# Attention and two feed-forward layers on one Trainium2 core: which PSUM banks the later pairs' flips, spreads and weighted sums use, and which engine subtracts the reloaded inputs' low parts

## The chip, the cores and the metric

One core of a Trainium2 chip runs the whole program. The metric is device time in microseconds (us); of the kernel before, three runs took 1277.73, 1278.05 and 1278.85 us, median 1278.05.

## What is computed

For 4 batches of 12 heads, 448 positions and 64 channels: q and k are normalised (RMS norm with gains), scores = q k^T / 8, softmax over the keys, times v. The result, 1792 tokens of 768 channels, goes through two layers. The first is x @ w_in (to 2048), relu, g = s * r * r + b, g @ w_out (back to 768). The second is h = x @ w_in, g = h * cos(h), g @ w_out.

```
attn = softmax(scale * rmsnorm(q) @ rmsnorm(k).T); x = attn @ v
x = (s * relu(x @ w1_in)**2 + b) @ w1_out
h = x @ w2_in; out = (h * cos(h)) @ w2_out
```

All inputs and outputs are float32; the layers' weights are stored as 64-bit floats and turned into 32-bit floats by bit operations in the kernel. Each operand of the layers' products is split in a high and a low part, and three matmuls (high by high, high by low, low by high) give one product.

## The kernel before, in words

Attention goes by pairs of heads: 24 pairs, six to a batch. A pair has four steps, one for each quarter of the queries (112 of 448). A step makes two score tiles, one per head (`scores`, L223): VectorE takes the negative maximum of each (L246), ScalarE the exponential (L254). Two steps later `turn` (L264) transposes the weights into two tiles that ScalarE (first head, L278) and VectorE (second head, L276) copy out. Once in a pair, `flip` (L190) transposes the next pair's normalised q (in the pair's second step) and k (third step), copied out in `unflip` by ScalarE (L211) and VectorE (L213); and for the pair before, in the third step, `spread` (L280) transposes the reciprocal sums into a tile that ScalarE copies (L286), and `mix` (L288) makes the weighted sum of v in 16 matmuls, which VectorE multiplies by the spread in `finish` (L303) a step later.

PSUM has eight banks, and each of these tiles takes one: two under the tag "mo", which the layers' matmuls use too (hidden tiles ph, output tiles po), two under "tp" and four under "sc". A tile waits till the tile that had its bank has been read. For the first nine pairs (`ALONE` = 9) attention runs alone, and flip, spread and sum take "mo"; from the tenth on the first layer's matmuls run between the steps and take "mo" for themselves, and `bank` (L185) sends flip, spread and sum to "tp", beside the turned weights. (A flip made for pair i asks `bank` with i - 2.) A score tile of step s also waits for the exponentials of step s - 2 by a dependency of its own (`follow`). TensorE's attention work is kept in the order in which it is written (`line`); all else is ordered by the compiler's list of priorities and its own estimate of times, so an order of instructions on an engine is fixed when the kernel is built.

The first layer is done in two passes: batches 0 and 1 while attention for the rest goes on, then batches 2 and 3. The attention output of batches 2 and 3 is written to DRAM and loaded again by `reload` (L576) when the weights come round: six column blocks of 128 x 448 for each batch. One block is a DMA into a tile xr of tag "t0" (two slots, shared with the hidden tiles' relu results), a cast on ScalarE to the high part xh (L98), and a subtraction that gives the low part xl (L99), both in `split` (L95). The subtraction is on VectorE for blocks 0, 1, 4 and 5 and on GpSimd for 2 and 3. The first layer's result for batches 0 and 1 is reloaded for the second layer in the same way. VectorE also converts the weights (L439 to L441), scales the squares (L479) and adds the output tiles into their accumulators (L525); GpSimd squares (L477) and makes most of the other low parts (L494, L401, L220).

Of the kernel before, what the change touches and what calls it, by code (L numbers as in the profile page):

```python
# [10 lines left out]
F32 = mybir.dt.float32  # L11
# [22 lines left out]
def body(ctx, tc, q, k, v, g_q, g_k, w1_in, w1_out, s_in, b_in, w2_in, w2_out, out):  # L34
    nc = tc.nc
# [3 lines left out]
    P = 128  # L39
# [53 lines left out]
    xs = {}  # L93

    def split(src, pool, key, eng=nc.gpsimd):  # L95
        hi = pool.tile([P, S], F32R, tag="xh", name=f"xh_{key}", bufs=2 * NE)
        lo = pool.tile([P, S], F32R, tag="xl", name=f"xl_{key}", bufs=2 * NE)
        nc.scalar.copy(hi, src)  # L98
        eng.tensor_tensor(lo, src, hi.bitcast(F32), ALU.subtract)  # L99
        return hi, lo  # L100
# [12 lines left out]
    def attention(keep):  # L113
        att, ps = pools["att"], pools["ps"]
# [70 lines left out]
        def bank(i, name):  # L185
            if i < ALONE:
                return psm.tile([P, 512], F32, tag="mo", name=name, bufs=2)
            return ps.tile([P, 512], F32, tag="tp", name=name)

        def flip(i, nm):  # L190
            b, hp = pairs[i]
            pt = bank(i - 2, f"pt_{nm}_{b}_{hp}")[:, :S]
            src = st[i]["q by chunk"] if i == 0 and nm == "q" else st[i]["n" + nm]
            mm = [nc.tensor.transpose(pt[:, c * CP:(c + 1) * CP], src[:, c, :, :].rearrange("p h d -> p (h d)"), ident[:CP, :CP]) for c in range(NCH)]
            line("PE", mm[0], mm[-1])
            st[i]["p" + nm] = pt
# [83 lines left out]
        def spread(i):  # L280
            b, hp = pairs[i]
            rt = bank(i, f"rt_{b}_{hp}")[:, :S]
            mm = [nc.tensor.transpose(rt[:, c * CP:(c + 1) * CP], st[i]["rb"][:, c, :, :].rearrange("p h d -> p (h d)"), ident[:CP, :CP]) for c in range(NCH)]
            line("PE", mm[0], mm[-1])
            x = st[i]["x"] = att.tile([P, S], F32, tag="xf", name=f"xf_{b}_{hp}")
            line("ACT", nc.scalar.copy(x, rt))  # L286

        def mix(i, part):  # L288
            b, hp = pairs[i]
            if part[0] == 0:  # L290
                st[i]["pa"] = bank(i, f"av_{b}_{hp}")[:, :S]
            mm = []
            for kc in part:
                for j in range(2):
                    mm.append(nc.tensor.matmul(st[i]["pa"][j * D:(j + 1) * D, :], st[i]["v"][:, j, kc, :], st[i]["pT", j][:, kc, :], start=(kc == 0), stop=(kc == NCH - 1)))  # L295
            line("PE", mm[0], mm[-1])
            for z in mm[1:]:
                issue_after(z, mm[0])
# [277 lines left out]
    def reload(layer, b, c, pool):  # L576
        t = ma.tile([P, S], F32, tag="t0", name=f"xr_{layer}_{b}_{c}")
        nc.sync.dma_start(t, stash[layer, b, c])
        xs.setdefault((layer, b), []).append(split(t, pool, f"{layer + 1}_{b}_{c}", nc.vector if c % 4 < 2 else nc.gpsimd))

    segs = [(0, (0,), [0]), (0, (0, 1), range(1, NCK)), (0, (1,), [0]), (0, (2, 3), range(NCK)), (1, (0, 1, 2, 3), range(NCK))]
    L2 = 4
# [69 lines left out]
    for n, u in enumerate(units):  # L652
# [14 lines left out]
        if soon:  # L667
            reload(*soon.pop(0))
        elif again and n % 4 == 0:
            reload(*again.pop(0))  # L670
        if u[0] == "in":
            while soon and len(xs.get((u[1], u[5]), [])) < NE:
                reload(*soon.pop(0))
            while again and u[1] == 1:
                reload(*again.pop(0))
        for cost in (unit_in if u[0] == "in" else unit_out)(*u[1:]):
            debt += cost * rates[min(seg, 1)]
            while debt > 0:
                c = next(steps, None)
# [34 lines left out]
```

## Time and profile before

| | |
|---|---|
| median of three runs | 1278.05 us |
| the profiled execution's own time | 1284.1 us |
| its span | 1282.3 us |
| TensorE busy | 1245.4 us (97%) |
| VectorE busy | 861.2 us (67%) |
| ScalarE busy | 757.0 us (59%) |
| GpSimd busy | 619.8 us (48%) |
| mean granted TensorE clock | 0.995 |

The profile is of one execution. Its times count from the first instruction. "PE" is TensorE, "PEld" its weight loads, "DVE" VectorE, "ACT" ScalarE, "POOL" GpSimd, "SP" the engine whose queue issues the DMAs. In a timeline a row is one or several like instructions: start, time taken, engine, line, operation, out<-in, and in square brackets how long the engine had stood and what ended that. Matmuls overlap, so their times add up to more than the time that passes; the distance of their starts is the better measure. A granted clock of 1.00 is 2.4 GHz, one of 0.50 is 1.2 GHz.

### The profile page before, as it was taken

The numbers are of one execution on the slowest core, as the hardware profiler recorded it, in microseconds if no ns is written. First come the engines' busy times: TensorE is split into PE (matmuls) and PEld (weight loads), VectorE is DVE, ScalarE is ACT, GpSimd is POOL, SyncE is SP. The second block draws the span as 40 slices with busy tenths as digits, with TensorE's granted clock in tenths as the row PEclk, the third lists the DMA queues.
The fourth block names the chain that finished last, engine by engine and source line by source line (L and its number), as shares of the span: only waits on it lengthen the run. The fifth ranks groups of instructions, "written<-read, shape, count | busy, mean of one in ns | idle before, by whom it ended". The sixth has DMA issues, their size and how long they took to land.

```text
span 1282.3 us, 19021 instructions
## 1 busy us (share of the span) xinstructions
PE 1245.4 (97%) x6788; PEld 1051.2 (82%) x6788; DVE 861.2 (67%) x1456; ACT 757.0 (59%) x1704; POOL 619.8 (48%) x673
## 2 busy tenths in 40 slices
PE   7999998999999999999999999999999999999998
PEld 5544676678777776789999999998999999999998
DVE  6888768876877866743444447854767766676755
ACT  5778878766666655525332226787656657565640
POOL 5566857565474642424332223665443535354531
PEclk9999999999999999999999999999999999999999
DMA  4333324533443322542221212211212111111205
GB/s 128 97 97 105 113 79 127 167 122 117 151 119 112 120 89 71 158 145 86 92 64 50 62 45 74 74 39 59 61 41 74 50 50 50 50 50 50 62 1 173
DMA packets 82223, 111.34 MB, mean 87 GB/s; under 512 B 8112, under 2 KB 72144, under 8 KB 82128
## 3 DMA queue, kind: packets, MB, share of 16 engines
q1 hardware_dynamic: 82128, 110.13, 28.3%
q8 instruction: 53, 0.87, 0.3%
q14 instruction: 42, 0.34, 0.1%
HBM read 86.51 MB, written 23.59 MB: 86 GB/s over the span
## 4 chain that ended last, share of the span: by engine, by line
PE 58%; DVE 10%; ACT 7%; DMA 2%; POOL 2%; issue 2%; DVEq 0%; ACTq 0%; POOLq 0%
PE ph L464 24%; PE po L543 14%; PE po L516 14%; PE av L295 2%; DVE t L440 2%; PE tp L272 2%; DVE gt L488 2%; DVE gt L489 2%; PE sc L233 2%; DVE t L441 1%; DMA xr<-xd 1%; ACT gh L493 1%; ACT gt L490 1%; DVE c L439 1%; DVE gt L479 1%
## 5 line engine op out<-in xcount | busy, mean ns | idle before, releaser
L464 PE MATMUL ph<-xl,wh 128*128 128x448 f32 x768 | 283.0, 369 | 0.0
L464 PE MATMUL ph<-xh,wl 128*128 128x448 f32 x768 | 283.0, 368 | 0.0
L464 PE MATMUL ph<-xh,wh 128*128 128x448 f32 x768 | 280.4, 370 | 0.5 <-ACT r L475 0.5
L494 POOL TENSOR_TENSOR gl<-gt,gh 128x448 fp32r<-128x448 f32 x128 | 152.7, 1197 | 177.4 <-ACT gh L493 177.3
L516 PE MATMUL po<-gh,wh 128*128 128x448 f32 x384 | 146.8, 384 | 9.8 <-DVE acc L525 8.4
L401 POOL TENSOR_TENSOR wl<-t,wh 128x384 fp32r<-128x384 f32 x128 | 140.4, 1111 | 32.5 <-ACT wh L398 31.3
L464 PEld LDWEIGHTS ph<-xl,wh 128*128 128x128 f32 x768 | 144.2, 188 | 14.0 <-issue 2.0
L464 PEld LDWEIGHTS ph<-xh,wh 128*128 128x128 f32 x768 | 144.1, 188 | 13.8 <-issue 1.3
L543 PE MATMUL po<-wh,gh 128*128 128x384 f32 x448 | 152.0, 340 | 2.4 <-ACT acc L549 1.2
L464 PEld LDWEIGHTS ph<-xh,wl 128*128 128x128 f32 x768 | 144.3, 188 | 12.2 <-issue 1.0
L398 ACT CAST wh<-t 128x384 fp32r<-128x384 f32 x200 | 95.2, 512 | 97.5 <-PE po L516 48.7
L525 DVE TENSOR_TENSOR acc<-po,acc 128x448 f32<-128x448 f32 x168 | 102.8, 618 | 74.2 <-PE po L516 73.7
L543 PE MATMUL po<-wl,gh 128*128 128x384 f32 x448 | 149.8, 335 | 0.4 <-POOL wl L401 0.4
L543 PE MATMUL po<-wh,gl 128*128 128x384 f32 x448 | 149.8, 334 | 0.0
L551 DVE TENSOR_TENSOR acc<-po,acc 128x384 f32<-128x384 f32 x196 | 105.3, 550 | 61.0 <-PE po L543 61.0
L254 ACT ACTIVATE pr<-sc,top 112x448 f32<-112x448 f32 x184 | 116.2, 637 | 49.1 <-DVE top L246 48.6
L516 PE MATMUL po<-gl,wh 128*128 128x448 f32 x384 | 142.8, 372 | 0.0
L516 PE MATMUL po<-gh,wl 128*128 128x448 f32 x384 | 142.7, 372 | 0.0
L492 POOL TENSOR_TENSOR gt<-hs,gt 128x448 f32<-128x448 f32 x64 | 78.5, 1227 | 128.7 <-ACT gt L491 113.6
L493 ACT CAST gh<-gt 128x448 fp32r<-128x448 f32 x128 | 71.2, 564 | 96.0 <-DVE gt L479 57.0
L477 POOL TENSOR_TENSOR r<-r 128x448 f32<-128x448 f32 x64 | 65.7, 1027 | 125.5 <-ACT r L475 118.6
L440 DVE SCALAR_TENSOR_TENSOR t<-c,t 128x384 uint32<-128x384 uint32 x128 | 96.2, 755 | 38.7 <-ACT t L436 35.8
(101 smaller groups left out, 2386.2 us busy)
## 6 DMA issues: line engine op xcount, KB each, us to landing
raw<-in_moe_w_in_dram SPq DMA_DIRECT2D x64, 384.0 KB, 3.5
raw<-in_moe_w_out_dram SPq DMA_DIRECT2D x64, 384.0 KB, 3.2
t<-wd SPq DMA_DIRECT2D x72, 192.0 KB, 2.4
wd<-t SPq DMA_DIRECT2D x64, 192.0 KB, 2.7
rawk<-in_k_dram SPq DMA_DIRECT2D x24, 224.0 KB, 3.5
rawv<-in_v_dram SPq DMA_DIRECT2D x24, 224.0 KB, 2.9
rawq<-in_q_dram SPq DMA_DIRECT2D x23, 224.0 KB, 3.0
xd<-xf SPq DMA_DIRECT2D x12, 224.0 KB, 2.6
```

The lines of the kernel that those rows point to most:

```text
L254: e = line("ACT", nc.scalar.activation(pr, sc[j], AF.Exp, bias=tops[j], scale=scale[j], accum_out=st[i]["sums"][:, c, j:j + 1]))
L398: z = nc.scalar.copy(wh, w)
L401: eng.tensor_tensor(wl, w, wh.bitcast(F32), ALU.subtract)
L440: nc.vector.scalar_tensor_tensor(t, c, 0x80000000, t, ALU.bitwise_and, ALU.bitwise_or)
L464: nc.tensor.matmul(h, a, m, start=(c == 0 and n == 0), stop=(c == NE - 1 and n == 2))
L492: nc.gpsimd.tensor_tensor(gt, h, gt, ALU.mult)
L493: nc.scalar.copy(gh, gt)
L494: nc.gpsimd.tensor_tensor(gl, gt, gh.bitcast(F32), ALU.subtract)
L516: marks["out"] = nc.tensor.matmul(po, a, m, start=(f == 0 and n == 0), stop=(f == CF - 1 and n == 2))
L525: nc.vector.tensor_tensor(at, po, at, ALU.add)
L543: nc.tensor.matmul(po, a, m, start=(f == 0 and n == 0), stop=(f == CF - 1 and n == 2))
L551: nc.vector.tensor_tensor(at, po, at, ALU.add)
```

## The change

`bank` gives flips, spreads and weighted sums from the tenth pair on a tile of the tag "sc", in the same ring of four as the scores, instead of one of the tag "tp"; the "tp" ring keeps the turned weights alone. `reload` gives the low parts to VectorE only for the second layer; for the first layer's second pass (batches 2 and 3) all six blocks go to GpSimd.

```
         def bank(i, name):
             if i < ALONE:
                 return psm.tile([P, 512], F32, tag="mo", name=name, bufs=2)
-            return ps.tile([P, 512], F32, tag="tp", name=name)
+            return ps.tile([P, 512], F32, tag="sc", name=name, bufs=4)
...
     def reload(layer, b, c, pool):
         t = ma.tile([P, S], F32, tag="t0", name=f"xr_{layer}_{b}_{c}")
         nc.sync.dma_start(t, stash[layer, b, c])
-        xs.setdefault((layer, b), []).append(split(t, pool, f"{layer + 1}_{b}_{c}", nc.vector if c % 4 < 2 else nc.gpsimd))
+        xs.setdefault((layer, b), []).append(split(t, pool, f"{layer + 1}_{b}_{c}", nc.vector if layer and c % 4 < 2 else nc.gpsimd))
```

## Rows read from the trace of the kernel before

**Rows 1.** The page: busy time by engine, and the exponentials' group.
```profile
PE 1245.4 (97%) x6788; PEld 1051.2 (82%) x6788; DVE 861.2 (67%) x1456; ACT 757.0 (59%) x1704; POOL 619.8 (48%) x673
...
L254 ACT ACTIVATE pr<-sc,top 112x448 f32<-112x448 f32 x184 | 116.2, 637 | 49.1 <-DVE top L246 48.6
```

**Rows 2.** Windows: stretch, length, busy time (instructions) by engine, clock, DMA share, GB/s.
```profile
160.00:200.00 40.00, 39.01 (x242) 28.88 (x240) 26.19 (x46) 29.23 (x73) 20.55 (x29) 1.00 0.27 82
200.00:240.00 40.00, 34.12 (x179) 25.39 (x179) 36.42 (x58) 30.08 (x76) 29.91 (x30) 0.91 0.55 172
...
520.00:560.00 40.00, 36.03 (x169) 29.75 (x169) 24.83 (x38) 14.10 (x29) 14.89 (x14) 0.96 0.54 170
```

**Rows 3.** Waits of TensorE, whole span: us in total, times, longest.
```profile
PE po L516 <- DVE acc L525: 8.4, 9, 2.2
...
PE sc L233 <- ACT pr L254: 3.0, 2, 2.3
```

**Rows 4.** Timeline of TensorE: four stalls of spread, sum and turned weights.
```profile
150.96 0.60 PE L283 MATMUL rt<-ident,rb 112*128 112x112 f32 x4 [1.03 <-DVE pT L276]
...
195.16 3.23 PE L295 MATMUL av<-pT,rawv 112*64 112x448 f32 x16 [0.42 <-DVE pT L276]
...
220.66 0.60 PE L283 MATMUL rt<-ident,rb 112*128 112x112 f32 x4 [3.14 <-DVE pT L276]
...
233.00 0.60 PE L272 MATMUL tp<-ident,pr 112*112 112x112 f32 x4 [0.78 <-DVE xf L303]
```

**Rows 5.** 206 to 236.2 us: window, timeline of VectorE, chain of waits.
```profile
206.00:236.20 30.20, 25.11 (x133) 18.50 (x133) 29.06 (x43) 21.03 (x52) 25.75 (x23) 0.94 0.54 171
...
221.40 0.61 DVE L525 TENSOR_TENSOR acc<-po,acc 128x448 f32<-128x448 f32 x1
...
233.53 0.48 DVE t L441
```

**Rows 6.** Window behind the longest stall, and the chain in a clean stretch.
```profile
222.40:224.60 2.20, 2.20 (x7) 1.67 (x6) 2.20 (x3) 0.51 (x2) 2.20 (x3) 0.50 0.01 3
...
569.05 14.26 PE ph L464 x69
```

**Rows 7.** Timelines of TensorE, VectorE and ScalarE, 541 to 555 us.
```profile
541.96 0.47 PE L516 MATMUL po<-gh,wh 128*128 128x448 f32 x1 [1.15 <-DVE acc L525]
...
548.10 0.62 DVE L99 TENSOR_TENSOR xl<-xr,xh 128x448 fp32r<-128x448 f32 x1 [2.78 <-ACT xh L98]
548.64 1.15 DVE L525 TENSOR_TENSOR acc<-po,acc 128x448 f32<-128x448 f32 x2
...
549.31 0.47 PE L516 MATMUL po<-gh,wh 128*128 128x448 f32 x1 [2.23 <-DVE acc L525]
...
549.63 0.57 ACT L98 CAST xh<-xr 128x448 fp32r<-128x448 f32 x1 [1.56 <-DMA xr<-xd]
...
554.63 0.37 PE L464 MATMUL ph<-xh,wh 128*128 128x448 f32 x1
```

**Rows 8.** Line L99 (ns: least, median, most), and the second reload's window.
```profile
L99 DVE TENSOR_TENSOR xl<-xr,xh x16: 607/624/1406, 481.7 to 649.3; 128x448 fp32r<-128x448 f32 x16
...
L99 POOL TENSOR_TENSOR xl<-xr,xh x8: 1128/1148/1302, 486.4 to 642.2; 128x448 fp32r<-128x448 f32 x8
...
532.00:554.00 22.00, 18.03 (x78) 15.32 (x77) 12.50 (x22) 6.83 (x14) 5.76 (x5) 0.92 0.56 175
```

**Rows 9.** Timelines of TensorE and ScalarE: a score's start, its second exponential.
```profile
499.43 0.46 PE L233 MATMUL sc<-kh,qh 64*112 64x448 f32 x2
...
501.67 0.62 ACT L254 ACTIVATE pr<-sc,top 112x448 f32<-112x448 f32 x1
```

**Rows 10.** Line L440 (ns: least, median, most); accumulations from 532 to 554 us.
```profile
L440 DVE SCALAR_TENSOR_TENSOR t<-c,t x128: 540/559/1893, 44.4 to 1222.5; 128x384 uint32<-128x384 uint32 x128
...
L525 DVE TENSOR_TENSOR acc<-po,acc 128x448 f32<-128x448 f32 x12 | 7.2, 618 | 3.3 <-PE po L516 3.2
```

More of the change, by code (lines that the diff above doesn't have):

```diff
@@ L187, in bank @@
                 return psm.tile([P, 512], F32, tag="mo", name=name, bufs=2)
-            return ps.tile([P, 512], F32, tag="tp", name=name)
+            return ps.tile([P, 512], F32, tag="sc", name=name, bufs=4)
         def flip(i, nm):
@@ L578, in reload @@
         nc.sync.dma_start(t, stash[layer, b, c])
-        xs.setdefault((layer, b), []).append(split(t, pool, f"{layer + 1}_{b}_{c}", nc.vector if c % 4 < 2 else nc.gpsimd))
+        xs.setdefault((layer, b), []).append(split(t, pool, f"{layer + 1}_{b}_{c}", nc.vector if layer and c % 4 < 2 else nc.gpsimd))
     segs = [(0, (0,), [0]), (0, (0, 1), range(1, NCK)), (0, (1,), [0]), (0, (2, 3), range(NCK)), (1, (0, 1, 2, 3), range(NCK))]
```

## The prediction

> **What bounds the kernel now.** I read the page's busy times first: TensorE is busy for 1245.4 of 1282.3 us [rows 1], so what a change of waits can give lies in the 37 us in which it stands still, and in stretches in which its clock was lowered. The table by windows says where [rows 2]: between 200 and 240 us TensorE works 34.12 of 40 us and its granted clock is 0.91; between 520 and 560 us it works 36.03 us at 0.96. (Full speed is 1.00, 2.4 GHz; the dips are stretches at the lower level, 1.2 GHz.) Both windows lie in the stretch that the edit touches, about 120 to 560 us, where attention runs between the matmuls of the first layer. Then TensorE's list of waits [rows 3]: the longest is the output matmuls behind VectorE's accumulation (8.4 us). The timeline then shows each stall with the instruction that ended it.
>
> **Part 1, the banks.** Before, the ring "tp" of two banks serves, for each pair from the tenth on, eight turned tiles, two flips, a spread and a weighted sum. Each needs the bank of the tile two before it, so flip, spread and sum wait for a copy that was only just asked for. Seven stalls are of this kind, of which four stand in [rows 4]: the five before 206 us, from 1.03 down to 0.24 us (the other three are flips and a spread of 0.24 to 0.33), together 2.35 us; the two at 220.66 and 233.00 us are 3.14 and 0.78, together 3.92 us. After, the four tiles that aren't turned weights come from the ring of four. Twelve tiles a pair over four banks give a fixed pattern: a spread takes the bank of the second score tile of one step earlier, the sum that of the k flip. By the times of this trace those banks were long free, so the seven stalls go.
>
> Does it reach the end? Between 160 and 200 us VectorE is busy 26.19 of 40 us [rows 2], so it can follow: I keep 2.35 us. From 206 to 236.2 us it is busy 29.06 of 30.2 us [rows 5], and the chain of waits runs through its weight conversion at 233.53 us: TensorE is ahead of it. Take the 3.14 us away, and the output matmuls behind the spread are late next: their bank is freed by the accumulation that VectorE reaches only at 221.40 us, behind the same conversions. So VectorE's own idle time, 1.14 us, is about what can be won while its work stays the same. The ends are 0 and 3.92 us; I take 1.1, since the nearest row is the full VectorE. The clock: 0.91 over 40 us is 3.6 us of full-speed work lost. From 222.4 to 224.6 us it is 0.50 [rows 6], and one matmul takes about twice the 14.26 / 69 = 0.207 us of a clean stretch [rows 6]; TensorE had stood for 3.14 us just before. If VectorE goes on holding it, it will still stand: ends 0 and 3.6 us, I take 0.
>
> The ring of four has a cost. Score tiles waited for exponentials of two steps before; now at three of four steps a bank comes from the step just before. A score started at 499.43 us has its second exponential done at 502.29 us, 2.86 us later [rows 9]. Steps are mostly 4 to 10 us apart there, and only a few (2 to 3 us) are closer. The trace has two waits of scores for exponentials, 3.0 us in all, in steps as close [rows 3]. What waits behind such a score is all of TensorE. Ends: 0 and 12.6 us (fifteen waits of one exponential, 0.637 us [rows 1] and its 0.2 us read, worked out below); I take 0.3 us lost. No instruction is added in this part, and the copies that free the banks stay on ScalarE and VectorE.
>
> **Part 2, the low parts.** For batches 2 and 3, columns 0, 1, 4 and 5, eight subtractions move from VectorE (624 ns) to GpSimd (1148 ns) [rows 8]. VectorE takes its instructions in order: at 548.10 us it does such a subtraction after 2.78 us of standing, for the high part, which ScalarE gives once the input's DMA has landed (the last one at 549.63 us). The accumulation behind it, at 548.64 us, frees the bank for which TensorE waits till 549.31 us, 2.23 us; the same before 541.96 us, 1.15 us [rows 7]. After, VectorE accumulates as soon as the matmuls are done. I keep the 2.23 us. Of the 1.15 us I keep half, 0.6: what is late next there is a weight's low part, whose high part stands on ScalarE behind the high parts of the inputs (ends 0 and 1.15). The clock in this window is 0.96 over 40 us, 1.6 us lost, right behind the 2.23 us stall; from 556 us on nothing stops TensorE, so I count 1.5 of it.
>
> What it costs: 8 x 1.148 = 9.2 us on GpSimd, which is busy 5.76 of 22 us in the second of the two reloads [rows 8]. Behind them in its queue stand squares and low parts of the hidden layer; each can be held up to 1.15 us, and by the wait for the input's high part longer. The two slots for loaded inputs are freed 0.52 us later a time; with three loads through each, the last low part comes at most 1.6 us later, and the loads' DMAs, in order on SP, with it. The twelve DMAs stay the same in number. The last would be there at 549.63 + 0.57 + 1.15 = 551.35 us [rows 7, 8], with the 1.6 us at 552.95. The hidden matmuls that read it begin at 554.63 us [rows 7] with the first column; its own column is the last of six, at least 15 x 0.207 = 3.1 us later, so 557.7, and 553.4 when moved up by 4.3 us. It is there in time, if barely: I cost it at 0, without that cover 1.6 us.
>
> One row speaks against the move: VectorE's conversion L440 takes 540 ns at best and 1893 at worst, so something stretches it [rows 10]. The accumulations don't show that: 618 ns each in the second reload, beside GpSimd's work [rows 10]. The Trainium skill, page "SBUF — State Buffer", section "Who interferes with whom", says that a VectorE instruction with two SBUF inputs and a GpSimd instruction that reads SBUF block each other for the whole instruction; by it each moved subtraction can cost a conversion beside it 1.15 us, by estimate up to 9.2 us of VectorE. Since accumulations are what TensorE waits for, I take none of this into the sum.
>
> **Sum.** 2.35 + 1.1 - 0.3 for the banks, 2.23 + 0.6 + 1.5 for the low parts: 7.5 us. The profiled execution took 1284.1 us, so 1276.6 by its own time. The median of the runs shown is 1278.05, 6.0 us less; the same 7.5 us off gives **1270.6 us**. Some of the stalls may belong to the profiled execution alone, which is a reason for a range that reaches further up.
>
> **Rivals.**
> A. The forecast, 1270.6, own range 1267 to 1275: chance 0.52.
> B. Everything is kept: VectorE's queue is laid out anew as well, the clock never drops. 6.27 + 3.6 for the banks, 2.23 + 1.15 + 1.6 for the low parts, 14.9 us: 1263.2. For it: TensorE alone is full afterwards. Against it: 29.06 of 30.2 us. Chance 0.13.
> C. Given back: VectorE holds the first stretch and gives nothing there, and in the second the late inputs (a DMA, ScalarE behind it, now GpSimd) hold the hidden matmuls instead of the outputs; 2.35 less 1.6 is left, 0.8 us: 1277.3. Also where the compiler's new order eats the gain. Chance 0.20.
> D. Slower: scores wait for the step just before. It decides where steps come closer than 2.86 us. There are 15 pairs with three such steps; if a third of the 45, fifteen, lose one exponential (0.84 us), that is 12.6 us against the gain of 7.5: 1283.1. For it: a bank of scores is now held by whatever stands in ScalarE's queue. Against it: most steps are far enough apart. Chance 0.15.
>
> About 0.2% (2.6 us) is what a measurement of this kernel can tell from no change. Faster: nearly all of A and B and a little of C, 0.68; same 0.18; slower 0.14. The range 1263 to 1279 holds A, most of B and C.
>
> **What would show it.** In the changed profile no spread, flip or sum should wait for a copy of turned weights; the stalls at 220.66 and 233.00 us should be replaced by waits of output matmuls for VectorE's accumulation or be gone; TensorE should wait less for accumulation between 530 and 556 us and that window's clock should be 1.00; eight more subtractions on GpSimd at about 1.15 us. I am wrong if scores wait for exponentials by more than some 3 us in all, if hidden matmuls wait for low parts around 550 us, or if 200 to 240 us keeps its 5.9 idle us and the later window too.

## The result, and the profile after

The changed kernel took 1297.31 us (median of six runs, 1293.95 to 1300.95) beside 1279.13 us for the kernel before (six runs): a ratio of 1.0133, with a 95% interval of 1.0105 to 1.0162. It is slower by about 17 us; 1270.6 was forecast, and the range ended at 1279. The profiled execution of the changed kernel took 1293.95 us, its span is 1292.1 us, its mean granted clock 0.994.

First the page: TensorE's busy time. It answers to [rows 1].

```profile
PE 1264.0 (98%) x6788; PEld 1056.1 (82%) x6788; DVE 860.2 (67%) x1448; ACT 756.6 (59%) x1704; POOL 628.9 (49%) x681
```

TensorE runs the same 6788 matmuls and is busy for 18.6 us more, and it stands still for less (28.1 us against 36.9). Eight instructions have gone from VectorE to GpSimd, as the edit says. So the loss is no wait. The list of TensorE's waits (us in total, times, longest) says the same, beside [rows 3]:

```profile
PE tp L272 <- ACT pT L278: 6.3, 11, 2.1
PE tp L272 <- DVE pT L276: 3.3, 2, 2.1
PE sc L233 <- ACT pr L254: 3.0, 2, 2.3
...
PE po L516 <- DVE acc L525: 1.6, 2, 1.3
```

Scores wait for exponentials 3.0 us in two waits, exactly as before. The output matmuls wait 1.6 us for accumulations where it was 8.4. The two long new waits are those of turned weights, and they stand where VectorE is full, as the timeline of TensorE from 206 to 236 us shows in its only two stalls:

```profile
231.58 0.60 PE L272 MATMUL tp<-ident,pr 112*112 112x112 f32 x4 [2.09 <-ACT pT L278]
...
234.27 0.99 PE L272 MATMUL tp<-ident,pr 112*112 112x112 f32 x4 [2.09 <-DVE pT L276]
```

Where the loss is, the windows show. Columns as in [rows 2]; the first fence is the kernel after, the second the kernel before in a stretch that had not been shown.

```profile
200.00:240.00 40.00, 35.82 (x187) 25.86 (x186) 36.13 (x57) 29.63 (x73) 27.12 (x28) 0.91 0.52 161
...
440.00:480.00 40.00, 40.00 (x229) 29.05 (x229) 25.13 (x47) 22.04 (x54) 14.57 (x17) 1.00 0.35 107
...
520.00:560.00 40.00, 36.20 (x164) 31.41 (x163) 26.05 (x38) 17.27 (x36) 23.92 (x23) 0.96 0.49 146
```

```profile
440.00:480.00 40.00, 40.00 (x244) 32.15 (x242) 26.89 (x50) 25.36 (x62) 18.72 (x20) 1.00 0.31 97
```

Between 440 and 480 us both kernels show TensorE busy for 40.00 of 40 us at full clock; the one before runs 244 matmuls in it, the one after 229. TensorE does less in the same busy time. Which matmuls those are, the groups by line of TensorE show, from 120 to 560 us, shapes kept apart (group | busy time, mean ns | idle before); first before, then after:

```profile
L233 PE MATMUL sc<-kh,qh 64*112 64x448 f32 x120 | 27.5, 455 | 0.7 <-ACT pr L254 0.7
L233 PE MATMUL sc<-kl,qh 64*112 64x448 f32 x120 | 22.2, 365 | 0.0
L233 PE MATMUL sc<-kh,ql 64*112 64x448 f32 x120 | 22.0, 362 | 0.0
```

```profile
L233 PE MATMUL sc<-kh,qh 64*112 64x448 f32 x120 | 42.9, 459 | 0.7 <-ACT pr L254 0.7
L233 PE MATMUL sc<-kh,ql 64*112 64x448 f32 x120 | 33.3, 394 | 0.0
L233 PE MATMUL sc<-kl,qh 64*112 64x448 f32 x120 | 30.4, 376 | 0.0
```

The first row's mean is nearly the same (455 and 459 ns), its busy time is 15.4 us longer. A group's busy time counts a moment once in which two of its matmuls run: before, 120 matmuls of 455 ns fit into 27.5 us, two at a time; after, many run by themselves. A step of the timeline shows it. Before:

```profile
240.93 0.46 PE L233 MATMUL sc<-kh,qh 64*112 64x448 f32 x2
241.22 0.37 PE L233 MATMUL sc<-kh,ql 64*112 64x448 f32 x2
241.43 0.37 PE L233 MATMUL sc<-kl,qh 64*112 64x448 f32 x2
241.73 0.47 PE L516 MATMUL po<-gh,wh 128*128 128x448 f32 x1
```

After:

```profile
252.41 0.45 PE L233 MATMUL sc<-kh,qh 64*112 64x448 f32 x1
252.78 0.47 PE L516 MATMUL po<-gh,wh 128*128 128x448 f32 x1
253.09 0.36 PE L516 MATMUL po<-gh,wl 128*128 128x448 f32 x1
253.29 0.37 PE L516 MATMUL po<-gl,wh 128*128 128x448 f32 x1
253.59 0.45 PE L233 MATMUL sc<-kh,qh 64*112 64x448 f32 x1
253.59 0.65 PE L233 MATMUL sc<-kh,ql 64*112 64x448 f32 x2
253.88 0.56 PE L233 MATMUL sc<-kl,qh 64*112 64x448 f32 x2
254.38 0.40 PE L272 MATMUL tp<-ident,pr 112*112 112x112 f32 x2
```

A step's six score matmuls, three for each head, use 64 rows each. Before, they stand together, run in three pairs and take 241.73 - 240.93 = 0.80 us. After, the first head's first matmul is alone: 0.37 us till the next matmul starts, three output matmuls follow, then the other five, 254.38 - 253.59 = 0.79 us. The step is **parted**: it costs one lone matmul, and two more changes between output and score matmuls. The matmul ahead of a change, 253.29 to 253.59, takes 0.30 us where a plain one takes 0.20 (253.09 to 253.29), and so does the one behind it, 252.78 to 253.09. In the order as compiled none of the 60 steps from the tenth pair on is parted before, and 39 are after.

A sum over the trace's records from 118 us on, from each matmul's start to the next one's, with what TensorE stood still set apart, closes the account (a number with a colon counts the matmuls). It puts the kernel after (1293.95 us) beside a second profile of the kernel before (1277.6 us), whose late matmuls are spaced alike (see the end):

```
                                         before        after     change
score matmuls                             48.6          63.8      +15.2
layer matmuls next to a score     26:     8.0   121:   37.6       +9.9  (29.6 less 95 plain ones of 0.207)
layer matmuls next to other
  attention work                 179:    45.4    78:   19.7       -4.8  (-25.7 plus 101 plain ones)
turned weights, spreads, sums            109.4         113.0       +3.6
standing still, over 0.05 us at a time    21.5          13.5       -8.0
all else, the plain pace among it                                  +0.3
first to last matmul                    1152.6        1168.8      +16.2
```

The stalls went, by 8.0 us. Parting the scores cost about 25; 4.8 came back at the other attention work, next to which 101 layer matmuls fewer stand, about as many as have come to stand next to scores (95). Some 1.8 us of the 25 belong to the lower clock and not to the parting: behind the two stalls at 231.58 and 234.27 us the low stretch goes on past 240 us, where the kernel before is back at full speed, and scores and their neighbours run in it. The windows, after and then before:

```profile
240.00:244.00 4.00, 4.00 (x21) 3.13 (x18) 1.98 (x4) 1.87 (x5) 0.59 (x1) 0.66 0.01 3
```

```profile
240.00:244.00 4.00, 4.00 (x27) 3.30 (x25) 3.32 (x6) 3.79 (x10) 3.12 (x3) 1.00 0.00 0
```

### The profile page after: what moved, and what is told of

The parts are those of the page before. It is cut to its first block, busy times and chain, and to the rows that moved or that the text cites. A ratio compares the mean times of both kernels' runs of the same rounds, so it can differ in the third digit from the quotient of the medians.

```text
span 1292.1 us, 19032 instructions
## 1 busy us (share of the span) xinstructions
PE 1264.0 (98%) x6788; PEld 1056.1 (82%) x6788; DVE 860.2 (67%) x1448; ACT 756.6 (59%) x1704; POOL 628.9 (49%) x681
## 4 chain that ended last, share of the span: by engine, by line
PE 69%; DVE 12%; ACT 11%; POOL 3%; DMA 3%; issue 2%; SPq 0%; DVEq 0%; ACTq 0%; POOLq 0%
PE ph L464 26%; PE po L516 15%; PE po L543 14%; PE sc L233 5%; PE av L295 4%; PE tp L272 4%; ACT pr L254 3%; DVE t L440 2%; DVE gt L488 2%; DVE gt L489 2%; DVE c L439 2%; DVE t L441 1%; DVE top L246 1%; DMA xr<-xd 1%; DMA raw<-in_moe_w_in_dram 1%
## 5 line engine op out<-in xcount | busy, mean ns | idle before, releaser
L401 POOL TENSOR_TENSOR wl<-t,wh 128x384 fp32r<-128x384 f32 x128 | 139.5, 1105 | 42.7 <-ACT wh L398 33.2
L246 DVE TENSOR_REDUCE top<-sc 112x1 f32<-112x448 f32 x192 | 111.9, 616 | 28.7 <-PE sc L233 28.3
```

Of the source, the lines that this page charges most:

```text
L246: line("DVE", nc.vector.tensor_reduce(tops[j], sc[j], axis=AX.X, op=ALU.max, negate=True))
L401: eng.tensor_tensor(wl, w, wh.bitcast(F32), ALU.subtract)
```

## The experiments

Two numbers were read from each trace. "The scores' line" is the time from each score matmul's start to the next matmul's start, summed from 118 us on, standing still included (49.3 us in the second profile of the kernel before, 63.8 in the first of the kernel after). "Parted" counts steps in the order as compiled. Where the texts on record name theories by letters, T and P are that the heads' scores lose each other's company (P as it stood after the fourth experiment), Q is that VectorE stands for ScalarE's casts in the reload, and D is the prediction's.

**The ring alone.** The kernel before, with the edit of `bank` only.

```
-            return ps.tile([P, 512], F32, tag="tp", name=name)
+            return ps.tile([P, 512], F32, tag="sc", name=name, bufs=4)
```

> The ring of four for flips, spreads and sums alone; the low parts stay as before. Theory T (the compiler puts other matmuls between the two heads' score matmuls, which then no longer run side by side; in the changed profile the scores' matmuls took 63.8 us of TensorE's time from 118 us on, against 49.3): the whole loss is here, ratio to before 1.012 to 1.019, and the scores' line takes about 64 us. Rival L (the low parts on GpSimd hold the layers up): faster than before by some 0.2 to 0.6%.

1297.57 us, ratio 1.0145 (1.0109 to 1.0180); the scores' line 62.8 us. The whole loss is the ring's.

**The low parts alone.** The kernel before, with the edit of `reload` only.

```
-... nc.vector if c % 4 < 2 else nc.gpsimd))
+... nc.vector if layer and c % 4 < 2 else nc.gpsimd))
```

> The eight low parts on GpSimd alone; the banks stay as before. Theory T: 3 to 5 us faster than before, ratio 0.996 to 0.998, by the waits for accumulation before 542 and 549 us and the lowered clock behind them. Rival L: ratio 1.010 or more.

1277.44 us, ratio 0.9994 (0.9975 to 1.0014): nothing, a miss. The profiled execution (1283.95 us) says the same beside the first profile of the kernel before (1284.1), whose late matmuls are spaced alike (0.206 us, see the end). Its timeline of all engines in the second reload, cut to one chain:

```profile
542.63 1.13 ACT L98 CAST xh<-xr 128x448 fp32r<-128x448 f32 x2 [4.40 <-DMA xr<-xd]
...
543.28 2.56 POOL L99 TENSOR_TENSOR xl<-xr,xh 128x448 fp32r<-128x448 f32 x2 [3.52 <-ACT xh L98]
...
543.66 0.92 ACT L398 CAST wh<-t 128x384 fp32r<-128x384 f32 x2
...
544.21 2.04 DVE L401 TENSOR_TENSOR wl<-t,wh 128x384 fp32r<-128x384 f32 x2 [1.41 <-ACT wh L398]
...
546.17 1.14 DVE L525 TENSOR_TENSOR acc<-po,acc 128x448 f32<-128x448 f32 x2
...
546.84 0.51 PE L516 MATMUL po<-gh,wh 128*128 128x448 f32 x1 [2.27 <-DVE acc L525]
```

VectorE no longer does the inputs' low parts, but in its order a weight's low part (L401) stands ahead of the accumulation. That needs a cast on ScalarE, which stands in ScalarE's order behind the input's cast, and this stood 4.40 us for its DMA. TensorE's stall is 2.27 us again. And the two L401 take 2.04 us beside the subtractions on GpSimd; in the kernel before, the same line in this reload took 1.03 us for two. They are not stretched alike; the line of L401 in this stretch (ns: least, median, most):

```profile
L401 DVE TENSOR_TENSOR wl<-t,wh x2: 639/1058/1477, 544.2 to 544.8; 128x384 fp32r<-128x384 f32 x2
```

The Trainium skill, page "SBUF — State Buffer", section "Who interferes with whom", says that a VectorE instruction with two SBUF inputs and a GpSimd instruction that reads SBUF block each other for the whole instruction. The rows agree: the second L401 took 1.48 us and ended at 546.25 us (544.21 + 2.04), 0.41 us behind the second subtraction (543.28 + 2.56 = 545.84), so most of the 0.52 us that one L401 took in the kernel before lies behind the end of that subtraction.

**Both heads' scores held for the step before.** The kernel after, with the first score matmul made to wait for both exponentials of one step before, where it was two.

```
-                follow(mm[0], exps[s - 2])
+                follow(mm[0], exps[s - 1 if i > ALONE else s - 2])
```

> The whole change, and from the eleventh pair on a step's first score matmul waits for the last exponential of the step before, so that both banks are free when it starts and the six matmuls stay together. Theory T: the scores' line is back at about 49 us, and the time within 0.4% of before (ratio 0.996 to 1.004). Rival W (what costs is that scores wait for the exponentials of the step before): this makes that wait longer, so at least as slow as the change, ratio 1.014 or more.

1282.16 us, ratio 1.0025 (1.0005 to 1.0044); parted 0, the scores' line 50.0 us. Four fifths of the loss are gone with the parting. Now the waits of TensorE are what rival D had foreseen:

```profile
PE sc L233 <- ACT pr L254: 9.6, 7, 2.6
PE po L516 <- DVE acc L525: 5.7, 6, 2.6
```

Scores wait 9.6 us in seven waits, 6.6 more than before, and TensorE's whole standing still is 21.0 us, as before (21.5). Held together, the ring gives its gain back as waits; left to the compiler, it gives it back, and more, as parted steps.

**The heads one after the other.** The kernel before, with the six matmuls issued three and three.

```
-            for n, (x, y) in enumerate(terms):
-                for j in range(2):
+            for j in range(2):
+                for n, (x, y) in enumerate(terms):
```

> The kernel before, with a step's three matmuls of the first head ahead of the three of the second, back to back. No bank and no wait changes. Theory T: six matmuls one behind the other instead of three pairs, some 0.4 us more in each of 60 steps, 20 to 30 us: ratio 1.016 to 1.024. Rival W: nothing waits longer, ratio within 0.2% of 1.

1275.26 us, ratio 0.9971 (0.9957 to 0.9985): a miss. The scores' line is 50.0 us, and TensorE's timeline shows why:

```profile
242.40 0.47 PE L233 MATMUL sc<-kh,qh 64*112 64x448 f32 x2
242.69 0.38 PE L233 MATMUL sc<-kh,ql 64*112 64x448 f32 x2
242.90 0.38 PE L233 MATMUL sc<-kl,qh 64*112 64x448 f32 x2
243.20 0.47 PE L516 MATMUL po<-gh,wh 128*128 128x448 f32 x1
```

Still 0.80 us a step. What counts is not that the heads alternate, but that the six stand together. The theory was narrowed to that: what costs is another matmul between them. TensorE stands still for 18.5 us here instead of 21.5, and its granted clock between 520 and 560 us is 1.00 instead of 0.96; together that is about the gain. Why the other order gives it was not followed up.

**Parting by hand.** The kernel before with its own banks; from the tenth pair on the turning of two steps earlier is issued between the first score matmul and the other five (`unflip` and `finish` are moved ahead of the scores for that).

```
-            line("PE", mm[0], mm[-1])
+            if i < ALONE:
+                line("PE", mm[0], mm[-1])
+            else:
+                line("PE", mm[0])
+                turn(s - LAG_T)
+                line("PE", mm[1], mm[-1])
...
```

> The kernel before with its banks, but in every step from the tenth pair on the eight transposes of the turned weights are issued between the first score matmul and the other five. Theory P (a score matmul of one head that stands alone among matmuls of all 128 rows costs some 0.37 us, since it no longer runs beside the other head's; adjacent ones run side by side in whatever order, as the run with the heads one after the other showed): the scores' line takes 49 + 60 x 0.37 = 71 us from 118 us on, and the ratio to before is 1.012 to 1.020. Rival O (the loss comes from the new order of the layers' matmuls or from the ring's waits, not from parted scores): ratio 0.997 to 1.004.

1293.72 us, ratio 1.0116 (1.0090 to 1.0142), with no bank changed; the scores' line 67.9 us. A step of it in TensorE's timeline:

```profile
252.73 0.45 PE L233 MATMUL sc<-kh,qh 64*112 64x448 f32 x1
253.11 0.59 PE L277 MATMUL tp<-ident,pr 112*112 112x112 f32 x4
```

The lone matmul takes 0.38 us here as well. All 60 steps are parted, but in 15 the lone matmul came right behind the five of the step before and had company; (67.9 - 49.3) / 45 = 0.41 us for each of the rest.

**The ring, with the heads one after the other.** The kernel after with the loops of the fourth experiment, so that a parted step falls into three and three.

```
-            for n, (x, y) in enumerate(terms):
-                for j in range(2):
+            for j in range(2):
+                for n, (x, y) in enumerate(terms):
```

> The whole change, with a step's three matmuls of the first head ahead of the three of the second. Where the compiler parts a step (29 of 60 steps as built) all three of each head stand alone. Theory P: such a step's scores take 2 x 0.79 us in place of 0.80, 29 x 0.78 = 22 us more than before, the scores' line about 71 us, ratio 1.017 to 1.024, slower than the change. Rival O: as the change, 1.010 to 1.016.

1299.01 us, ratio 1.0165 (1.0128 to 1.0201); the scores' line 70.9 us with only 29 steps parted, so (70.9 - 49.3) / 29 = 0.74 us each, twice that of a lone matmul: three run without company instead of one. The order that cost nothing while the six stand together (the fourth experiment) costs most once they are parted.

**Spreads alone on the ring of four.** The kernel before with

```
+            if name[:2] == "rt":
+                return ps.tile([P, 512], F32, tag="sc", name=name, bufs=4)
```

> The kernel before, with the spread alone in the ring of four; flips and sums stay in the ring of two. As built no step is parted. Theory P: the scores' line stays at 49 to 50 us, the stall of 3.1 us before the spread goes, ratio 0.995 to 1.000. Rival O (any sharing of the scores' ring costs): ratio over 1.003.

1275.35 us, ratio 0.9975 (0.9957 to 0.9993); parted 0, the scores' line 50.0 us. A ninth tile a pair in the ring of four parts nothing. The stall of 3.14 us ahead of the spread is gone, and one of 1.97 us stands ahead of the weighted sum instead:

```profile
220.24 4.92 PE L297 MATMUL av<-pT,rawv 112*64 112x448 f32 x16 [1.97 <-DVE pT L278]
```

**Flips alone on the ring of four.** The same with `if name[0] == "p":`.

> The kernel before, with the flips alone in the ring of four; spreads and sums stay in the ring of two. As built 16 of 60 steps are parted. Theory P: 16 x 0.37 = 6 us more in the scores' line (55 us), ratio 1.002 to 1.007. Rival O: no proportion to the parted steps; either near 1.013 or near 1.000.

1286.97 us, ratio 1.0062 (1.0038 to 1.0085); parted 16, the scores' line 57.4 us. That is 8.1 us more, and the ratio is 7.9 us.

**Spreads on the ring, heads one after the other.** The seventh and fourth together.

> A version meant to beat both: the kernel before with the spread alone in the ring of four, and a step's three matmuls of the first head ahead of the second's. As built no step is parted. Theory P: scores' line at 50 us; the gains of the two runs that had one part each (0.25 and 0.29%) overlap, since both shorten the stall before the spread: ratio 0.994 to 0.998. Rival O: 1.000 or more.

1275.21 us, ratio 0.9966 (0.9948 to 0.9985); parted 0, the scores' line 50.8 us. The two gains don't add up: each alone gave as much.

**Casts and low parts of the reload off ScalarE and VectorE.** The kernel before, with both done on GpSimd for the first layer's second pass (`split` gets the cast as an argument).

```
-        nc.scalar.copy(hi, src)
+        cast(hi, src)
...
-... nc.vector if c % 4 < 2 else nc.gpsimd))
+... nc.vector if layer and c % 4 < 2 else nc.gpsimd, nc.scalar.copy if layer else nc.gpsimd.tensor_copy))
```

> The kernel before, with the whole split of the twelve blocks of the second pass on GpSimd: the cast to the high part too. Theory Q (the low parts alone gained nothing because ScalarE, in order, stands at the cast till the input's DMA has landed, the weights' cast stands behind it, and VectorE stands at the weights' low part ahead of the accumulations): the stalls of output matmuls for accumulation between 540 and 550 us shrink from some 3 us to under 1, ratio 0.995 to 0.999. Rival S (GpSimd's work beside it stretches VectorE's low parts of weights, or the late low parts hold the hidden matmuls): ratio 1.000 to 1.004.

1273.73 us, ratio 0.9961 (0.9949 to 0.9972): the fastest of all, faster than both kernels. The window of the second reload, in the low parts' experiment and then here:

```profile
520.00:560.00 40.00, 37.15 (x176) 31.07 (x175) 24.52 (x36) 14.78 (x31) 21.01 (x18) 0.96 0.55 171
```

```profile
520.00:560.00 40.00, 38.93 (x189) 32.83 (x188) 25.77 (x37) 11.51 (x24) 24.32 (x25) 1.00 0.58 183
```

With nothing in ScalarE's order that waits for the reload's DMAs, TensorE runs 13 matmuls more in the same 40 us than in that experiment and its granted clock stays at 1.00. Not all of the 5 us need be the cast's: between 200 and 240 us, ahead of the reload, this execution has a clock of 0.96 where both profiles of the kernel before have 0.91, some 2 us of full-speed work, and the edit doesn't say why. VectorE's L401 is still stretched beside GpSimd, but ends in time:

```profile
547.10 2.08 DVE L401 TENSOR_TENSOR wl<-t,wh 128x384 fp32r<-128x384 f32 x2
```

**Both kernels profiled again**, on one chip, to see what of the first profiles repeats.

> A second look at the kernel before, for the scatter between executions: if its stalls of 3.1 and 2.2 us and the lowered clock behind them are there again, they belong to the kernel; theory P does not depend on it: scores' line 49 us.

> A second look at the changed kernel: theory P expects the scores' line at 63 to 65 us again, about 14 us over the kernel before, whatever the execution's total.

1277.6 and 1299.95 us. The longest stall of the kernel before is there again:

```profile
220.69 0.60 PE L283 MATMUL rt<-ident,rb 112*128 112x112 f32 x4 [3.16 <-DVE pT L276]
```

and so is the clock of 0.91 between 200 and 240 us: both belong to the kernel. The one near 549 us was 0.65 instead of 2.23, the one near 541 us 1.86 instead of 1.15: these vary. The scores' line of the kernel after is 63.9 us, as in its first profile (63.8).

The last experiments' gains together (spreads on the ring, heads one after the other, casts on GpSimd) were not tried.

## Why the prediction was wrong

**Right: the stalls of part 1 went.** None of [rows 4] is left: no spread, flip or sum waits for a copy. In the stretch of a full VectorE most of it was given back, as put: 3.14 + 0.78 us became 2.09 + 2.09, though on turned weights and not on output matmuls. In all TensorE stands still for 4.18 us between 200 and 240 us where it was 5.88, 1.7 us less beside the 1.1 forecast. The clock there stayed at 0.91, so the 0 taken for it was right as to a gain; behind 240 us a little was lost, as the windows above show. The sum of the two parts' stalls, 6.3 us, stands beside 8.0 measured; with the ring alone 16.4 us of 21.5 are left.

**Wrong: "The ring of four has a cost ... I take 0.3 us lost".** This is the step that failed: the term was put at 0.3 us, and it measured about 25 (some 23 without the lower clock). It looked for the cost of late banks in one form only, a wait of a score, and so it went by the two waits of 3.0 us in the trace of before, taken for waits of close steps; 2.31 us of them stand at 15.20 us, in the first pair, where the edit changes nothing. That number came out exactly and told nothing. With the ring of four shared, the second head's bank comes free later than the first's, and where the compiler reckons with that it sets other matmuls between the first head's score and the rest: 39 of 60 steps, 15.2 us for the scores and 9.9 us for matmuls next to them. "No instruction is added in this part" was true, but the sum took it for granted that each instruction keeps its neighbours, and so its duration. That parting alone costs this much is shown by the fifth experiment, and that the ring costs it almost only through parting by the third, seventh and eighth (0.25% is left in the third, where nothing is parted). That it is the second head's later bank that makes the compiler part them is argued from the code; the third experiment agrees with it, but the compiler's own estimates are in no trace.

**Rival D had the sign, but neither the size nor the mechanism.** It gave 1283.1 us, some 5 us slower, and 1297.31 was measured. It put 12.6 us on scores that wait, at 15 of 45 steps. As built there is no such wait. Where the wait was forced, in the third experiment, it cost 6.6 us, half of what D gave. Rival C named "the compiler's new order" in half a sentence, with no price; it was the whole result.

**Wrong: "After, VectorE accumulates as soon as the matmuls are done".** This took 4.3 us as won (2.23 + 0.6 + 1.5 for the clock), and the second experiment measured a ratio of 0.9994, 0.8 us. The 2.23 us were in part the one execution's: in the second profile of the kernel before that stall is 0.65. The term of 0.6 had named the next thing late, a weight's low part whose cast stands on ScalarE behind the inputs'. But it was applied to the smaller stall alone; it holds for the larger one just as well. In the changed kernel the waits for accumulation between 520 and 560 us did shrink, from 3.97 to 1.64 us, but other waits came, so that TensorE stood still for 3.80 us there, as before (3.97), and the clock, put at 1.00, stayed at 0.96. The bound that had been left out of the sum, conversions held up beside GpSimd, was there in small: two L401 in 2.04 us instead of 1.03. The tenth experiment shows that the chain through ScalarE's order was what held it: with the cast moved too, no stall is left between 540 and 550 us, that window's clock is 1.00, and up to 5 us are won.

**Right: what part 2 costs.** Hidden matmuls did not wait for low parts, and GpSimd had the time for them.

## What to carry to other kernels

Before giving a tile another ring, ask what the new time of its bank does to the order in which the compiler places instructions, not only to waits: where two matmuls that use half the rows run in company, tie the first to what the second needs, as the third experiment did. Count starts, not busy time: an engine that is 98% busy with the same instructions can have become slower. Before crediting the removal of a wait, follow the next instruction of the same engine back through every queue behind it, down to the DMA, since an engine in order only moves on to its next wait.

## What had not been expected of the hardware

Matmuls of 64 rows on the two halves run in company even when three of one half are issued ahead of three of the other (0.80 us for six, either way). By itself one takes 0.37 us to the next start, more than a matmul of 128 rows and the same 448 columns among its like (0.20 us); three of one half by themselves take 0.79 us in the sixth experiment, as long as six of both halves together. The change between 64 and 128 rows shows as some 0.1 us on each side (0.30 and 0.31 us instead of 0.20); the Trainium skill, page "TensorEngine Tiling (Array Packing)", section "Tiling Modes", says that a change of the tiling drains TensorE, and this agrees in kind; it gives no size.

Executions of one kernel differ by some 6 us in how closely plain matmuls follow each other: behind the last score, the median from start to start is 0.206 us in the profiled execution of the kernel before (1284.1 us) and 0.202 in its second (1277.6); for the kernel after 0.202 (1293.95) and 0.206 (1299.95). Alike by alike, the change costs 16.4 and 15.9 us. The granted clock, 0.994 to 0.995 in all four, doesn't show the difference; what makes it was not found. The 6 us by which the first profile stood above the median were nearly all this pace: its stalls are only 1.0 us longer than those of the second.
